# The six-expert part in three groups of 1024 tokens, with 512-column matmuls and results by channel

## The chip, the cores and the metric

The kernel runs on one core of a Trainium2 chip. The metric is the device time of one execution in microseconds, start to end; three executions of the kernel before are given. Besides them there is one execution recorded by the hardware profiler, whose span runs from the first to the last instruction.

## The reference

A decaying linear attention (4 batches, 8 heads, 768 steps, head size 48) produces 3072 tokens of 384 channels. They go into a layer of 8 experts:

```python
logits = x @ w_gate                       # 3072 x 384 by 384 x 8
P = np.exp(logits - logits.max())
for _ in range(8):                        # rows and columns scaled in turn
    P /= P.sum(1, keepdims=True) + 1e-09
    P /= P.sum(0, keepdims=True) + 1e-09
    P *= N / E
out = np.zeros((N, D))
for e in range(E):
    h = np.maximum(x @ w1[e], 0.0)        # 384 -> 1024
    out += P[:, e:e + 1] * (h @ w2[e])    # 1024 -> 384
```

All experts see all tokens; P weighs their results. P is known only when the last token is, since its columns run over all tokens.

## The kernel before

**Precision.** A float32 operand of a matmul is held as two halves of a shorter format, a high one and a low one (`hh` and `hl`, `xh` and `xl`, index 0 and 1 of X and of the weight tiles). Each matrix product is three matmuls: high by high, high by low, low by high.

**Two parts.** In the first part (up to 593 us) the attention runs in chunks of 256 tokens, and the matmuls of experts 0 and 1 (L263 to L293) fill TensorE in between, weights resident, moving operand of 256 columns in the first layer and 384 in the second. A planner (class `Plan`) puts all its operations in an order, by costs and ranks; a job's cost in microseconds is the second argument of `job`. The order is then written out as it stands. Results of experts 0 and 1 go to DRAM without P (`ye_d`).

**Six experts.** The second part does experts 2 to 7 in groups of `UN` = 768 tokens, four groups (`u`), each in 16 steps (`t`, `NT`); a step is three blocks of 128 hidden channels. Tokens of a group are split in two halves of 384 (`TH`, index `j`). The first layer of a step, a 3x3 by 3x2 block product, is done with 15 products of 128x128 by 128x384 instead of 18, by sums of weight blocks and of X blocks formed beforehand; `PRODS` is their order, each adds to one of two PSUM banks A and B in turn, and after each product ScalarE copies the bank or VectorE adds it to or subtracts it from one of six running sums `s11` to `s32`. When a sum is complete, ScalarE writes relu's high half, and VectorE the low half (L1376, L1383). So a bank's content has to be read before the product after next, which goes to the same bank.

**Order in a step.** `step` writes the order out by hand: at position m from 1 to 15 there is the product, then its read, then the list `slots[m]` of other work, then one or two pieces (two at 5, 10 and 15) of the second layer of the step before. A piece is one block of hidden channels for 128 tokens: hidden values are the stationary operand, weights of 384 columns the moving one, three matmuls (L1277 to L1279) into one of six PSUM accumulators. When an expert's eight blocks are done, the accumulator is evicted: in group 0, when P isn't known yet, ScalarE copies it and it goes to DRAM; in the others it is multiplied by P per token and added up in SBUF (L1250, L1252).

**What lies in the slots.** In group 0 the weight sums of the next step (`prep_w`), written to DRAM too (`w_d`) and read back by the later groups (`fetch_w`); the eight scalings of P (`gating`, one round per step), which take a PSUM bank at a step's end for a small matmul; forming X of the next group in the last steps (`load_x`), into tiles that come free by and by; and in the later groups the joining of group 0's stored results (`late`, `join`) and of experts 0 and 1 (`fetch`, `mixin`). Weight tiles hold four to a step: a and b and a part of c the 15 sums, the rest of c and all of d the second layer. There are 10 (`WIDE`) for this part.

**The opening.** X of group 0, the weights of the first two steps and the first 15 products are planned into the first part's end (`opening`), between the last matmuls of experts 0 and 1.

All DMAs are issued from SyncE's queue, in program order. TensorE, VectorE and ScalarE each run their own instructions in program order.

Of the kernel before, what the change touches and what calls it, by code (L numbers as in the profile page):

```python
# [18 lines left out]
CH = 128  # L19
# [6 lines left out]
WIDE = 10  # L26
# [3 lines left out]
UN = 768  # L30
# [96 lines left out]
class Net:  # L127
# [9 lines left out]
    def build(self):  # L137
# [3 lines left out]
        with ExitStack() as ctx:  # L141
            dram = ctx.enter_context(tc.tile_pool(name="dram", bufs=1, space=DR))
            cst = ctx.enter_context(tc.tile_pool(name="cst", bufs=1))
            self.wp = ctx.enter_context(tc.tile_pool(name="wp", bufs=WIDE))
            self.psA = ctx.enter_context(tc.tile_pool(name="psA", bufs=2, space=PS))
# [22 lines left out]
            self.ye_d = [[dram.tile([128, C], F32, name=f"ye_d{u}_{i}") for i in range(self.ntt) if u < 2 or i < NS * NCH] for u in range(E)]  # L168
# [88 lines left out]
    def experts(self, i):  # L257
# [37 lines left out]
        for e in range(2):  # L295
            for f in range(NF):
# [4 lines left out]
                job("PE", 1.07, lambda e=e, f=f, p=p: first(e, f, p), xr + w1, [b], 10 * n)  # L301
# [14 lines left out]
    def phase1(self, c1, ca):  # L316
# [4 lines left out]
        self.wy = c1.enter_context(tc.tile_pool(name="wy", bufs=RING - WIDE))  # L321
# [44 lines left out]
        self.xs, self.plan, self.expert, self.seconds = {}, Plan(), set(), {}  # L366
# [360 lines left out]
    def opening(self, K):  # L727
# [9 lines left out]
        self.X, self.W, self.raw, self.home, self.H = {0: {}}, {}, {}, {}, {}  # L737
        self.nraw, self.nprep, self.want = [0, 0], 0, None
        X, t, L = self.X[0], {}, {}

        def tile(tag, name, wr=False):
            return (self.wr if wr else self.xa).tile([128, TH], F32, tag=tag, name=name)

        ring = ["y0", "y1", "xs", "mo0", "my0", "mo1", "my1"]
# [6 lines left out]
        def whole(k, c, j):  # L751
            tag = turn()

            def load():
                t[c, j], L[c, j] = tile(f"oa{k}", f"xt0{c}{j}_0"), tile(tag, f"xt1{c}{j}_0", tag == "xs")
# [3 lines left out]
            job("SP", 0.9, load, (), [("oa", k), ("low", tag)], land=6.0, kb=384)  # L759
            job("DVE", 0.475, lambda: V.tensor_tensor(t[c, j], t[c, j], L.pop((c, j)), ADD), [("low", tag)], [("oa", k), ("x", c, j)])  # L760

        def new(n):
            tag = spot[n]
            X[n] = self.xa.tile([128, 2, TH], F32R, tag=tag, name=f"X{n}_0")
            self.home[0, n] = (self.xa, tag)
            return X[n]

# [858 lines left out]
```

## Time and profile before

| | |
|---|---|
| median of three runs | 1706.25 us (1702.0 to 1706.36) |
| profiled execution, span | 1699.2 us; the page gives no other time of it, and the runs lie 2.8 to 7.2 us above its span |
| TensorE busy | 1672.3 us, 98%, 13776 matmuls |
| VectorE busy | 1281.3 us, 75% |
| ScalarE busy | 803.1 us, 47% |
| GpSimd busy | 8.9 us |
| DMA, mean share of the 16 engines | 59% |
| part with six experts | 593.5 to 1693.6 us |

Matmuls overlap in their records (one of 384 columns is shown with 334 ns and the next starts 173 ns after it), so their rate is read from starts, not from durations. The same holds for VectorE: its recorded durations are longer than the distance of two starts.

### The profile page before, as it was taken

The page shows a single profiled execution, that of the slowest core. Times are in us where ns is not written, and L with a number is a line of the kernel's source. Part 1 is how long each engine was busy: PE and PEld are TensorE (multiplying, and loading weights), DVE is VectorE, ACT ScalarE, POOL GpSimd, SP SyncE. Part 2 cuts the span into 40 slices and gives each one's busy share as a digit, 9 for nine tenths or more (in the row PEclk, how much of TensorE's full clock was granted, in tenths as well). Part 3 has the DMA queues.
Part 4 walks back from the last instruction along what each step waited for, and adds up shares of the span by engine and source line. Part 5 has one row for each costly group of instructions (what it writes and reads, how often), then busy time and mean ns, then how long its engine had stood idle before and what let it go on. Part 6 is the DMA issues. An engine that isn't in the chain of part 4 may idle for free.

```text
span 1699.2 us, 35042 instructions
## 1 busy us (share of the span) xinstructions
PE 1672.3 (98%) x13776; PEld 1631.4 (96%) x13776; DVE 1281.3 (75%) x2942; ACT 803.1 (47%) x1866; POOL 8.9 (1%) x20
## 2 busy tenths in 40 slices
PE   6999999999999999999999999999999999999998
PEld 3899999999999999999999999999999999999998
DVE  8899989999994989999854767665566766465665
ACT  7766656656553655555543333333333333333332
POOL 1000000000000000000000000000000000000000
PEclk9999999999999999999999999999999999999999
DMA  7445555445545888788875565666465566555460
GB/s 228 124 116 136 125 131 130 118 118 131 130 105 151 261 320 299 272 277 293 305 263 215 198 229 193 257 239 240 178 224 204 214 250 222 211 193 211 183 245 35
DMA packets 163469, 338.79 MB, mean 199 GB/s; under 512 B 14880, under 2 KB 122848, under 8 KB 163296
## 3 DMA queue, kind: packets, MB, share of 16 engines
q1 hardware_dynamic: 162496, 336.08, 59.0%
q8 instruction: 110, 1.80, 0.4%
q14 instruction: 63, 0.52, 0.1%
q10 hardware_dynamic: 800, 0.39, 0.1%
HBM read 236.27 MB, written 81.20 MB: 187 GB/s over the span
## 4 chain that ended last, share of the span: by engine, by line


## 5 line engine op out<-in xcount | busy, mean ns | idle before, releaser
L1376 ACT ACTIVATE hh<-s 128x384 fp32r<-128x384 f32 x378 | 198.9, 526 | 413.7 <-DVE s L1372 373.2
L1372 DVE TENSOR_TENSOR s<-s,A 128x384 f32<-128x384 f32 x315 | 174.0, 552 | 139.5 <-PE A L1358 137.0
L1279 PE MATMUL po<-w_d,hl 128*128 128x384 f32 x768 | 256.6, 334 | 0.0
L1278 PE MATMUL po<-w_d,hh 128*128 128x384 f32 x768 | 256.6, 334 | 0.0
L1277 PE MATMUL po<-w_d,hh 128*128 128x384 f32 x768 | 256.6, 334 | 0.0
L1383 DVE SCALAR_TENSOR_TENSOR hl<-s,hh 128x384 fp32r<-128x384 f32 x378 | 208.7, 552 | 6.1
L267 PE MATMUL ph<-xh,w 128*128 128x256 f32 x576 | 165.7, 288 | 1.2 <-ACT hl L273 0.8
L269 PE MATMUL ph<-xh,w 128*128 128x256 f32 x576 | 162.3, 282 | 0.0
L268 PE MATMUL ph<-xl,w 128*128 128x256 f32 x576 | 162.2, 282 | 0.0
L1369 ACT ACTIVATE s<-B 128x384 f32<-128x384 f32 x189 | 92.9, 491 | 117.7 <-PE B L1358 114.4
L1372 DVE TENSOR_TENSOR s<-s,B 128x384 f32<-128x384 f32 x189 | 104.1, 551 | 53.9 <-PE B L1358 51.6
L1277 PEld LDWEIGHTS po<-w_d,hh 128*128 128x128 f32 x768 | 144.2, 188 | 0.0
L1278 PEld LDWEIGHTS po<-w_d,hh 128*128 128x128 f32 x768 | 144.2, 188 | 0.0
L1279 PEld LDWEIGHTS po<-w_d,hl 128*128 128x128 f32 x768 | 144.2, 188 | 0.0
L273 ACT ACTIVATE hh<-ph 128x256 fp32r<-128x256 f32 x192 | 73.5, 383 | 131.2 <-PE ph L269 130.7
L285 PE MATMUL po<-w,hh 128*128 128x384 f32 x384 | 131.6, 343 | 0.0
L286 PE MATMUL po<-w,hh 128*128 128x384 f32 x384 | 128.9, 336 | 0.0
L287 PE MATMUL po<-w,hl 128*128 128x384 f32 x384 | 128.8, 336 | 0.0
L1279 PE MATMUL po<-w_c,hl 128*128 128x384 f32 x384 | 128.3, 334 | 0.0
L1278 PE MATMUL po<-w_c,hh 128*128 128x384 f32 x384 | 128.3, 334 | 0.0
L1277 PE MATMUL po<-w_c,hh 128*128 128x384 f32 x384 | 128.3, 334 | 0.0
L1391 DVE TENSOR_TENSOR s<-s,B 128x384 f32<-128x384 f32 x63 | 34.9, 554 | 115.7 <-PE B L1358 115.7
(258 smaller groups left out, 4075.7 us busy)
## 6 DMA issues: line engine op xcount, KB each, us to landing
w_d<-w_d SPq DMA_DIRECT2D x64, 768.0 KB, 7.2
w_a<-w_d SPq DMA_DIRECT2D x48, 768.0 KB, 4.3
w_b<-w_d SPq DMA_DIRECT2D x48, 768.0 KB, 5.7
w_c<-w_d SPq DMA_DIRECT2D x48, 768.0 KB, 6.3
raw<-in_w_dram SPq DMA_DIRECT2D x32, 576.0 KB, 5.8
w_d<-w_a SPq DMA_DIRECT2D x16, 768.0 KB, 3.2
w_d<-w_b SPq DMA_DIRECT2D x16, 768.0 KB, 5.0
w_d<-w_c SPq DMA_DIRECT2D x16, 768.0 KB, 6.3
```

What stands on the lines that cost most here:

```text
L267: nc.tensor.matmul(p, w[:, 0, cs], xh[:, ct, :], start=(ct == 0), stop=False)
L268: nc.tensor.matmul(p, w[:, 0, cs], xl[:, ct, :], start=False, stop=False)
L269: nc.tensor.matmul(p, w[:, 1, cs], xh[:, ct, :], start=False, stop=(ct == NCT - 1))
L285: nc.tensor.matmul(o, hh[:, s], w2h, start=f == 0, stop=False)
L286: nc.tensor.matmul(o, hh[:, s], w2l, start=False, stop=False)
L287: nc.tensor.matmul(o, hl[:, s], w2h, start=False, stop=f == NF - 1)
L1277: nc.tensor.matmul(po[k], hh[:, s], w2[:, 0], start=c == 0, stop=False)
L1278: nc.tensor.matmul(po[k], hh[:, s], w2[:, 1], start=False, stop=False)
L1279: nc.tensor.matmul(po[k], hl[:, s], w2[:, 0], start=False, stop=c == NF - 1)
L1372: V.tensor_tensor(S[nm], S[nm], ps, op)
L1376: A.activation(hh, S[nm], AF.Relu)
L1383: V.scalar_tensor_tensor(hl, S[nm], 0.0, hh.bitcast(F32), ALU.max, ALU.subtract)
```

## The change

Groups of the six-expert part get 1024 tokens (`UN`), so there are three, and halves 512. All products and second-layer matmuls have a moving operand of 512 columns.

The second layer turns its operands round: a block of 128x128 weights is stationary, the hidden values of 512 tokens move, and the result stands by channel. A piece is now one block of hidden channels, one half of tokens and one third of the channels; `TURNS` is the order of (block, half) in a step. The factors of P can't be applied per partition at the eviction any more. They are written to DRAM by token (`g_d`) and loaded, the same in every partition, as a tile per expert and half; in groups 1 and 2 VectorE multiplies them in right after a sum is complete (maximum with 0, then the factor), and ScalarE copies the high half from that. With that, an accumulator can run over all six experts in PSUM and is evicted once per group. In group 0 it is evicted per expert as before, and joined later with factor tiles (`pull`, `join`).

Results of experts 0 and 1 still stand by token; they are mixed by token, transposed in blocks of 32 on VectorE and stored so that DRAM holds them by channel (`mix`, `b_d`), and are the base to which groups add. The output leaves by channel, and the host's rearrangement at the end restores its order.

X of a group exists once. The sums of the next group are formed from step 3 on and stored to DRAM (`forms`, `xf_d`); in the last step of a group each X tile is rewritten right after the product that used it last. Weight tiles become 8; the four others of the ring of the first part hold four X tiles of three planes, whose third planes are low halves of the hidden values. The second half of d is therefore made at the beginning of the next step.

```diff
-WIDE = 10
+WIDE = 8
 LAG = 3
 TR = 4
 TB = 32
-UN = 768
+UN = 1024
 TH = UN // 2
 NS = UN // SUB
 NT = 6 * NF // 3
-NX = 15
+NX = 11
 WOPS = [2, 8, 6, 1, 12, 14, 3, 4, 7, 13, 10, 11, 0, 9, 5]
+ROWS = (1, 2, 0)
+TURNS = [(2, 1), (2, 0), (0, 0), (0, 1), (1, 1), (1, 0)]
...
+            self.u_d = {(e, k): dram.tile([128, TH], F32, name=f"u_d{e}_{k}") for e in range(2, E) for k in range(2 * NCT)}
+            self.b_d = [[dram.tile([C, TH], F32, name=f"b_d{u}_{j}") for j in range(2)] for u in range(self.N // UN)]
+            self.g_d = dram.tile([self.ntt, E, CH], F32, name="g_d")
...
+        ring = ["y0", "y1", "mo0", "xh", "xl", "my0"]
+        held = [self.firsts[self.N // (NCH * CH) - 2]]
...
+            if spot[n] < NX:
+                X[n] = self.xa.tile([128, 2, TH], F32R, tag=f"x{spot[n]}", name=f"X{n}_0")
+            else:
+                o = self.wy.tile([128, 3, TH], F32R, tag="w", name=f"X{n}_0")
+                X[n] = o[:, :2]
+                self.tail.append(o[:, 2])
             return X[n]
+
+        def lot(n):
+            k = spot[n] = len(spot)
+            return [self.seconds[1, k - NX]] if k >= NX else []
...
+        g = yield from bank([half, 2, CH])
+        for q in range(2):
+            nc.tensor.transpose(g[:, q], flat[:, half * q:half * q + half], self.ident)
+        V.tensor_copy(pt, g)
+        nc.sync.dma_start(self.g_d.rearrange("(q t) e c -> (t e) q c", q=2), pt)
+        yield
...
+        def factor(o, u, j, e):
+            g = self.g_d[NS * u * NCH + j, e]
+            nc.sync.dma_start(wide(o), bass.AP(g.tensor, g.offset, [[0, 128], [NCH * E * CH, NS], [1, CH]]))
...
+        def mix(tt, part):
+            y0, y1 = Y[tt]
+            if part == 0:
+                A.activation(y0, y0, AF.Copy, scale=self.P[:, tt, 0:1])
+            elif part == 1:
+                V.scalar_tensor_tensor(y0, y1, self.P[:, tt, 1:2], y0, ALU.mult, ALU.add)
+            else:
+                m = late("m", f"m{tt}", None, C)
+                V.transpose(m, y0)
+                u, r = divmod(tt, NS * NCH)
+                s, j = divmod(r, NCH)
+                for b in range(4):
+                    nc.sync.dma_start(self.b_d[u][j][:, s * CH + 32 * b:s * CH + 32 * b + 32].rearrange("(q a) b -> a q b", a=32), m[32 * b:32 * b + 32].rearrange("a (q b) -> a q b", b=32))
...
+        def join(q):
+            if q >= len(pairs):
+                return
+            k, e = pairs[q]
+            (y, g), o = J.pop((k, e)), J["o", k]
+            V.tensor_tensor(y, y, g, ALU.mult)
+            V.tensor_tensor(o, o, y, ALU.add)
+            if e == E - 1:
+                nc.sync.dma_start(result(0, k), wide(o))
...
-            if e == 2:
-                oa[tt] = self.xa.tile([128, C], F32, tag=f"oa{k}", name=f"oa{tt}")
-                A.activation(oa[tt], po[k], AF.Copy, scale=self.P[:, tt, 2:3])
-            else:
-                V.scalar_tensor_tensor(oa[tt], po[k], self.P[:, tt, e:e + 1], oa[tt], ALU.mult, ALU.add)
-            if e == E - 1:
-                nc.sync.dma_start(self.out[tt * CH:tt * CH + CH, :], oa[tt])
+            o = oa[u, k]
+            V.tensor_tensor(o, o, po[k], ALU.add)
+            nc.sync.dma_start(result(u, k), wide(o))
...
+            for i, j in TURNS:
+                for c in range(NCT):
+                    yield u, 2 + (3 * t + (i + 1) % 3) // NF, u * NT + t, i, j, NCT * j + c
...
-            nc.tensor.matmul(po[k], hh[:, s], w2[:, 0], start=c == 0, stop=False)
-            nc.tensor.matmul(po[k], hh[:, s], w2[:, 1], start=False, stop=False)
-            nc.tensor.matmul(po[k], hl[:, s], w2[:, 0], start=False, stop=c == NF - 1)
-            if c == NF - 1:
+            c = k % NCT
+            nc.tensor.matmul(po[k], w2[:, 0, c], hh, start=f == 1, stop=False)
+            nc.tensor.matmul(po[k], w2[:, 0, c], hl, start=False, stop=False)
+            nc.tensor.matmul(po[k], w2[:, 1, c], hh, start=False, stop=f == last)
...
+            if 1 < n < NT:
+                _, hi, lo, _ = prep[n]
+                slots[1] += [hi(5)]
+                slots[4] += [lo(5)]
+            elif n >= NT:
+                slots[1].append(lambda: self.fetch_w(n, [3]))
+            if n + 1 < NT:
+                def begin():
+                    prep[n + 1] = self.prep_w()
+
+                slots[1].append(begin)
+
+                def do(q, *a):
+                    return lambda: prep[n + 1][q](*a)()
+
+                slots[1] += [do(0, 0, 3)]
+                slots[2] += [do(0, 3, 8)]
+                slots[3] += [do(0, 8, 13), do(1, 0)]
+                slots[4] += [do(1, 1)]
+                slots[5] += [do(2, 0)]
+                slots[6] += [do(1, 2), do(1, 3), do(2, 1)]
+                slots[7] += [do(2, 2), do(2, 3)]
+                slots[9] += [do(1, 4)]
+                slots[13] += [do(2, 4)]
+            elif n + 1 < len(steps):
+                slots[1].append(lambda: self.fetch_w(n + 1, [0, 1]))
+                slots[6].append(lambda: self.fetch_w(n + 1, [2]))
...
+            if u + 1 < NU and t == NT - 2:
+                for q in range(3):
+                    slots[13 + q].append(lambda: (deal(len(jobs)), [ahead(u + 1) for _ in range(3 if jobs else 2)]))
+            if u + 1 < NU and t == NT - 1:
+                for m, (c, k) in enumerate(PRODS, 1):
+                    if k in self.plains:
+                        slots[m].append(lambda k=k: self.fetch_x(u + 1, k))
+                    else:
+                        slots[m].append(lambda k=k: A.activation(X[k][:, 0], queue[k], AF.Copy))
+                        (slots[m + 1] if m < 8 else carry).append(lambda k=k: (V.tensor_tensor(X[k][:, 1], queue[k], X[k][:, 0].bitcast(F32), ALU.subtract), ahead(u + 1)))
...
+                if t == 0 and u > 1:
+                    for k in range(2 * NCT):
+                        slots[1 + k].append(lambda k=k: ground(u - 1, k))
+                a, b = divmod(n - 1, NT)
+                if a and (3 * b + 3) // NF > 3 * b // NF:
+                    a, b = divmod((E - 2) * a + 3 * b // NF + 2, E - 2)
+                    if a < NU:
+                        slots[3].append(lambda: factors(a, 2 + b))
+                for m, q in zip((3, 6), joins(n)):
+                    slots[m].append(lambda q=q: join(q))
+                for m, q in zip((11, 13), joins(n + 1)):
+                    slots[m].append(lambda q=q: pull(q))
...
+                h[i, j] = halves(i, j, n)
+                if u:
+                    V.scalar_tensor_tensor(S[nm], S[nm], 0.0, G[u, 2 + (3 * t + (i + 1) % 3) // NF, j], ALU.max, ALU.mult)
+                A.activation(h[i, j][0], S[nm], AF.Copy if u else AF.Relu)
...
+                    if u:
+                        V.tensor_tensor(hl, S[nm], hh.bitcast(F32), ALU.subtract)
...
-                4: lambda ps: (add("s22", ps), high(1, 1, "s22")),
+                4: lambda ps: add("s22", ps),
                 0: lambda ps: (add("s12", ps, SUB), high(0, 1, "s12")),
-                6: lambda ps: (s21(ps), high(1, 0, "s21")),
+                6: s21,
             }
-            lowers.append(low(1, 0, "s21"))
+            lowers.append(lambda: (high(1, 0, "s21"), low(1, 0, "s21")()))
             slots[9].insert(0, low(2, 1, "s32"))
             slots[10].insert(0, low(0, 0, "s11"))
             slots[11].insert(0, low(2, 0, "s31"))
-            slots[14].insert(0, low(1, 1, "s22"))
-            slots[15].insert(0, low(0, 1, "s12"))
+            slots[14].insert(0, lambda: high(1, 1, "s22"))
+            slots[15][:0] = [low(1, 1, "s22"), low(0, 1, "s12")]
...
+            for k in range(2 * NCT):
+                ground(NU - 1, k)
...
-    out = nc.dram_tensor("out_0_dram", (N, C), F32, kind="ExternalOutput").ap()
+    out = nc.dram_tensor("out_0_dram", (N // CH, 128, NCT, CH), F32, kind="ExternalOutput").ap()
```

## Rows read from the trace of the kernel before

**Rows 1.** The page, section 1: busy us, share of the span, instructions.
```profile
PE 1672.3 (98%) x13776; PEld 1631.4 (96%) x13776; DVE 1281.3 (75%) x2942; ACT 803.1 (47%) x1866; POOL 8.9 (1%) x20
```

**Rows 2.** Table by stretches: us, busy us of each engine (started), PEclk, DMA share, GB/s.
```profile
600.00:700.00 100.00, 99.71 (x572) 98.27 (x572) 90.90 (x237) 55.31 (x112) 0.00 (x0) 1.00 0.85 305
...
1400.00:1500.00 100.00, 100.00 (x579) 100.00 (x578) 55.66 (x106) 36.90 (x72) 0.00 (x0) 1.00 0.58 219
```

**Rows 3.** Waits of TensorE, 590 to 1699 us: total, times, longest.
```profile
PE B L1356 <- DVE s L1372: 0.3, 1, 0.3
```

**Rows 4.** Timeline of TensorE: start us, us, operation; both ends of an undisturbed stretch.
```profile
1111.82 0.34 PE L1357 MATMUL B<-X,w_b 128*128 128x384 f32 x1
...
1248.75 0.34 PE L1279 MATMUL po<-w_d,hl 128*128 128x384 f32 x1
```

**Rows 5.** Timeline of TensorE in the two-expert part, seven periods apart.
```profile
514.80 0.28 PE L267 MATMUL ph<-xh,w 128*128 128x256 f32 x1
...
529.59 0.28 PE L267 MATMUL ph<-xh,w 128*128 128x256 f32 x1
```

**Rows 6.** Timeline of TensorE: first and last matmul of the six-expert part's steps.
```profile
593.50 0.33 PE L1356 MATMUL B<-X,w_b 128*128 128x384 f32 x1
...
1693.27 0.34 PE L1279 MATMUL po<-w_c,hl 128*128 128x384 f32 x1
```

**Rows 7.** Timeline of TensorE around one pair of the gating's matmuls.
```profile
699.31 0.34 PE L1279 MATMUL po<-w_d,hl 128*128 128x384 f32 x1
699.48 0.28 PE L1157 MATMUL g<-cs,ones 128*128 128x8 f32 x2
...
700.03 0.34 PE L1357 MATMUL B<-X,w_b 128*128 128x384 f32 x1
```

**Rows 8.** DMA issues: queue, count, KB each, median us to landing.
```profile
X<-x_d SPq DMA_DIRECT2D x32, 192.0 KB, 5.3
```

**Rows 9.** Timeline of VectorE, operations back to back.
```profile
557.48 0.55 DVE L777 TENSOR_TENSOR xs<-xt,xs 128x384 f32<-128x384 f32 x1
557.95 0.55 DVE L784 TENSOR_TENSOR X<-xs,X 128x384 fp32r<-128x384 f32 x1
...
565.98 0.95 DVE L1086 TENSOR_TENSOR w_a<-sum,w_a 128x768 fp32r<-128x768 f32 x1
566.85 0.42 DVE L277 TENSOR_TENSOR hl<-hf,hh 128x256 fp32r<-128x256 f32 x1
```

**Rows 10.** Groups of instructions by line and form: busy us, mean ns; idle before.
```profile
L1252 DVE SCALAR_TENSOR_TENSOR oa<-po,P,oa 128x384 f32<-128x384 f32 x90 | 53.7, 613 | 25.0 <-PE po L1279 25.0
```

**Rows 11.** Table by stretches: within group 0, and across groups 1 and 2.
```profile
700.00:820.00 120.00, 120.00 (x693) 119.71 (x693) 110.88 (x303) 66.15 (x133) 0.00 (x0) 1.00 0.78 274
...
1111.00:1249.00 138.00, 138.00 (x796) 137.53 (x794) 82.22 (x160) 50.51 (x99) 0.00 (x0) 1.00 0.61 224
```

**Rows 12.** Timelines of TensorE and VectorE: from product to read, and back.
```profile
618.33 0.33 PE L1358 MATMUL B<-X,w_a 128*128 128x384 f32 x1
618.70 0.56 DVE L1391 TENSOR_TENSOR s<-s,B 128x384 f32<-128x384 f32 x1 [1.28 <-PE B L1358]
...
622.48 0.55 DVE L1372 TENSOR_TENSOR s<-s,B 128x384 f32<-128x384 f32 x1
623.09 0.44 PE L1356 MATMUL B<-X,w_b 128*128 128x384 f32 x1 [0.25 <-DVE s L1372]
```

**Rows 13.** Table by stretches, the opening: first stretch and sum.
```profile
545.00:555.00 10.00, 10.00 (x76) 9.91 (x74) 3.02 (x8) 3.89 (x11) 0.00 (x0) 1.00 0.98 290
...
sum 48.00, PE 48.00 PEld 47.91 DVE 39.36 ACT 27.77 POOL 0.00; mean PE 9.60 PEld 9.58 DVE 7.87 ACT 5.55 POOL 0.00
```

**Rows 14.** DMA issues: the last stores.
```profile
out_dram<-oa SPq DMA_DIRECT2D x18, 192.0 KB, 1.9
```

**Rows 15.** Line of the raw weights' loads: durations, and time to landing.
```profile
L1035 SPq DMA_DIRECT2D raw<-in_w_dram x32: 383/406/1728, 527.7 to 820.5; - x32
...
DMA to landing us min/median/max: 4.3/5.8/7.9
```

More of the change, by code (lines that the diff above doesn't have):

```diff
@@ L875, in opening @@
         plain(11, *x31)
-        plain(0, *x22)
         raw(1)
@@ L879, in opening @@
         gates(1)
+        plain(0, *x22)
         lower(2)
@@ new lines, in run @@
+                o = self.xf_d[u, n] = self.dram.tile([128, TH], F32, name=f"xf_d{u}_{n}")
+                nc.sync.dma_start(o, low[f])
+            out.append(run)
+        ADD, SUB = ALU.add, ALU.subtract
+        r, l = regs, low
+        load(0, 0, 0, 0)
+        load(1, 0, 1, 1)
+        whole(0, 0)
+        whole(1, 1)
+        load(0, 1, 2, 1)
+        form(3, 0, r[0], r[1], SUB)
+        whole(2, 1)
+        form(8, 0, r[0], r[2], ADD)
+        form(12, 1, r[1], l[0], SUB)
+        load(1, 1, 3, 0)
@@ L1047, in prep_w @@
         self.nprep += 1
-        ts = self.slots(n)
+        ts = self.slots(n, range(2) if inline else range(4))
         raw = self.raw.pop((0, n))
@@ L1134, in gating @@
         cs = sp.tile([128, E], F32, name="cs")
+        half = self.ntt * E // 2
+        pt = sp.tile([half, 2, CH], F32, name="pt")
         V.tensor_reduce(mx, flat, AX.X, ALU.max)
@@ new lines, in base, with late, factors, fetch @@
+        def base(u, k):
+            j, c = divmod(k, NCT)
+            return self.b_d[u][j][c * 128:c * 128 + 128, :]
+        def late(tag, name, bufs=None, n=TH):
+            return more["pool"].tile([128, n], F32, tag=tag, name=name, bufs=bufs)
+        G = {}
+        def factors(u, e):
+            for j in range(2):
+                G[u, e, j] = late(f"g{j}", f"g{u}_{e}_{j}", 2)
+                factor(G[u, e, j], u, j, e)
+        Y = {}
+        def fetch(tt):
+            Y[tt] = [late(f"y{q}", f"y{q}_{tt}", 2, C) for q in range(2)]
@@ new lines, in phase2b, with pull @@
+        pairs = [(k, e) for k in range(2 * NCT) for e in range(2, E)]
+        J = {}
+        def pull(q):
+            if q >= len(pairs):
+                return
+            k, e = pairs[q]
+            if e == 2:
+                J["o", k] = late("jo", f"jo{k}")
+                nc.sync.dma_start(J["o", k], base(0, k))
+            J[k, e] = late("jy", f"jy{k}_{e}", 2), late("jg", f"jg{k}_{e}", 2)
+            nc.sync.dma_start(J[k, e][0], self.u_d[e, k])
+            factor(J[k, e][1], 0, k // NCT, e)
@@ L1287, in step @@
                 for i, j, nm in ((2, 1, "s32"), (1, 1, "s22"), (0, 1, "s12")):
-                    hh, hl = (hp.tile([128, TH], F32R, tag=f"{q}{i}{j}", name=f"{q}{i}{j}_0", bufs=2) for q in ("hh", "hl"))
+                    hh, hl = halves(i, j, 0)
                     A.activation(hh, self.sums[nm], AF.Relu)
@@ L1331, in deal @@
+            for m in (2, 4, 7, 8, 10, 12):
+                slots[m].append(lambda: next(gate, None))
             def deal(k):
```

414 lines of the change are left out of this document (190 added, 224 removed).

## The prediction

> **What bounds the kernel now.** I read the busy shares first, then the table by stretches, then TensorE's waits, and only then the order of single instructions. TensorE is busy for 1672.3 of 1699.2 us, VectorE for 1281.3 [rows 1]. A busy share alone proves little, because matmuls overlap; the table shows more: from 600 to 1600 us, 572 to 579 matmuls start in each 100 us, whatever the other engines do, and the granted clock is 1.00, that is 2.4 GHz [rows 2]. TensorE's waits between 590 and 1699 us that the profile can name sum to 0.3 us [rows 3]. So the six-expert part is bound by how fast matmuls follow one another. That rate has its own rows: between two undisturbed points 790 matmuls of 384 columns take 136.93 us, 173.33 ns each [rows 4]. 384 columns at 2.4 GHz are 160.0 ns; 13.3 ns per matmul are not columns.
>
> **The change part by part.**
>
> *Fewer, wider matmuls.* One step before issues 15 products and 18 second-layer pieces of three matmuls each, 99 matmuls of 384 columns, over 4 x 16 steps: 6336. After it is the same 99 per step, of 512 columns, over 3 x 16 steps: 4752. The columns are equal (2,433,024 both times), so what goes is the part of a matmul that isn't columns, 1584 times. No row has a 512-column matmul of this kind. The two nearest sizes are 384 and, in the two-expert part, 256: seven periods of nine 256-column and six 384-column matmuls last 529.59 - 514.80 = 14.79 us [rows 5], 2.113 a period; less 6 x 0.1733 there remain 1.073 for nine, 119.2 ns each, 12.5 over its 106.7 of columns. The excess hardly grows: 12.5 at 256, 13.3 at 384. Continued on that line it is 14.1 at 512 (pitch 227.4); held at 13.3 the pitch is 226.7. I take 227.0 between them. Before: 6336 x 0.17333 = 1098.2 us. After: 4752 x 0.2270 = 1078.7. **-19.5 us**; -17.5 and -21.1 at the two pitches. The far bound is an excess that grows with the columns: 173.33 x 512/384 = 231.1 ns and no gain at all.
>
> The Trainium skill (TensorE: Matmul & The Clock Gate, Back-to-back issue gap) says that warm matmuls follow one another after their columns at 2.4 GHz plus a fixed 2.5 ns or so. By that, an estimate from the page, the change would save only 1584 x 2.5 ns = 4.0 us. This trace has 13.3 ns where the page has 2.5 [rows 4], in a stream in which each matmul loads weights of its own, and the measurement decides.
>
> *What else TensorE loses.* From 593.50 to the end of the last matmul's turn (1693.27 + 0.17) are 1099.9 us [rows 6]; the 6336 - 45 matmuls issued there take 1090.4 of them, the other 45 being issued before, in the opening. Of the 9.5 left, the gating's own small matmuls take about 4: one such place goes from 699.31 to 700.03, 0.72 us where two plain turns are 0.35, so 0.37 [rows 7], and there are 11. The new transposes make it 12. The other 5 or so lie where groups change: three changes become two, about -1. New there: X is now one set, rebuilt in the last step of a group, ScalarE's copy directly after the product that used the tile, from a prefetch issued three products earlier, behind the last sums. A load of X took 5.3 us in the middle [rows 8]; from slot 13 of one step to slot 1 of the next are about 5.4, so the first copy may hold ScalarE by a microsecond, twice: +1 to +2. Sum **+1**, bounds -3 (all of the rest gone) and +4.
>
> *VectorE's load.* It is paid only if it makes TensorE wait. VectorE's turn is shorter than its recorded duration: 128x384 operations start 0.47 us apart, a 128x768 one 0.87 after which the next starts [rows 9], so 512 columns take 0.47 + 128 x 0.40/384 = 0.60. A step of groups 1 and 2 has 10 sums from PSUM, 6 low halves and, new, 6 gating products: 22 x 0.60 = 13.2 us. VectorE's evictions with the factor go (30 per group, 613 ns each [rows 10]; 6 more are ScalarE's); in their place there are 6 per group, 0.2 us a step. Joins of group 0 cost 72 operations over 21 steps, 3.4 x 0.60 = 2.1; mixing two of 0.47; forming X about 1.1. Sum 17.6 us in a step of 99 x 0.227 = 22.5: 78%. Group 0 before is busy for 110.88 of 120 us [rows 11], 16.0 of a 17.3 us step, and TensorE loses nothing but the gating's turns; its 16 operations of 384 columns grow by 0.13 each (2.1) and X takes about 1 more: 19.1 in 22.5, 85% where it was 92%. So the cover holds on average.
>
> What counts is each single read of PSUM. A product's bank is needed again ten matmuls after the start of its last one. Before that is 1.73 us; VectorE starts to read 0.37 us after that matmul starts, takes 0.55, and TensorE follows 0.06 after [rows 12], so a read may be 0.75 us late. After: 2.27 - (0.37 + 0.05 + 0.67 + 0.06) = 1.1 us. The new gating product stands directly behind the sum on VectorE, and the next read behind both. At positions 8 and 9 this makes 1.2 + 1.8 us of work in 2.7 of TensorE's, at 14 and 15 1.8 + 1.8 in 3.4: lag up to 0.4, less than 1.1. One step is worse, the first of group 2, where six evictions (3.6 us) and six late halves of X (3.6) fall in: 13.2 + 3.6 + 3.6 + 0.9 = 21.3 of 22.5, with a lag of about 1.2 at the last read. I put **+0.5** on it (0 to 3). The copies of relu's result on ScalarE now wait for VectorE's gating product; their readers stand a slot or more behind, and ScalarE is busy for only 50.51 of 138 us there [rows 11]. I cost it at nothing.
>
> *Opening.* After the last logits TensorE has 48 us of two-expert work and products, without a gap, while VectorE is 39.4 of 48 us busy [rows 13]. 33 operations become 0.13 us longer: 4.4 us. VectorE's idle time lies mostly ahead of 555 (3.0 of 10 us busy), where it waits for loads, and two of the temporaries now wait for the last-but-one chunk. Four of the X tiles wait for second-layer weights of the second expert; behind the fourth there are still four rounds of 2.1 us each. Cover is there, not much: **+1** (0 to +6).
>
> *Tail.* Last sum 0.1 us longer, and a store of 256 KB in 512-byte pieces where one of 192 KB in 1536-byte pieces took 1.9 us [rows 14]: **+0.6** (0 to +2).
>
> *At nothing:* weight traffic (3 MB a step, for 22.5 us instead of 17.3, so the DMA share of 0.61 [rows 11] falls), the order of weight rows, the extra output transposition, the two-expert part.
>
> Sum: -19.5 + 1 + 0.5 + 1 + 0.6 = -16.4. The profiled execution's span is 1699.2, and by this 1682.8 after; the runs shown lie 2.8 to 7.2 above that span, the median 7.05, so I take it from the median: 1706.25 - 16.4 = 1690.
>
> **Rivals.**
> *A, wider matmuls save nothing.* The excess grows with columns (231.1 ns). For it: no 512-column row. Against: 256 columns would then have 8.9 ns of excess and have 12.5. Time: 1706.25 + 3.1 = 1709. Chance 0.08. The Trainium skill's constant of 2.5 ns (the section named above) would give nearly the same, 1706.25 - 4.0 + 3.1 = 1705, an estimate from that page.
> *B, slower: VectorE's reads come late in groups 1 and 2.* It decides once a read lags more than 1.1 us. If at three places of each of the 32 steps (9, 10, 15) the product behind comes 0.4 us late, that is 38 us: 1728; from 0.22 us at each the gain is gone and the kernel is over the 0.3% bound. For it: two thirds of the steps get six more operations on VectorE in the very chain. Against: 78% load and a longer grace than before. Chance 0.07.
> *C, weights just in time.* With 8 weight tiles instead of 10, the second half of a step's second-layer weights is made at the start of the next step, and the raw load behind it has from slot 4 to slot 9. It starts about 1.8 us into slot 4 and is wanted 9.6 us after that slot's start: 7.8. Loads took 4.3, 5.8 in the middle, 7.9 at most [rows 15]. If it misses by 0.5 to 1 us in all 14 steps, +7 to +14: 1697 to 1704. Chance 0.08.
>
> **How the numbers follow.** Forecast 0.77, A 0.08, B 0.07, C 0.08. The forecast's own range is 1684 (-21.1, -1) to 1698 (-17.5, with the upper bounds of two of the other terms). The 8-in-10 range reaches over most of C: 1682 to 1703. About 0.3% (5 us) is what a measurement can tell from none; faster by more, that is under 1701: 0.77 + 0.06 of C = 0.83. Within: A and the end of C, 0.10. Slower: B, 0.07.
>
> **What would show it.** Right: the 512-column matmuls start 0.227 us apart, about 440 in 100 us; no wait of TensorE on VectorE over 1 us outside the first step of group 2 and the group changes; the last logits stay at about 545. Wrong: 0.231 apart (A); repeated waits of TensorE on sums at positions 9, 10 and 15 from about 950 us on (B); ScalarE waiting for raw weights in group 0 (C); a gap of TensorE at 590 to 600 (the opening).

## The result, and the profile after

After: 1728.0 us, the median of 4 runs (1722.49 to 1729.72), beside 1704.13 for the kernel before (1702.0 to 1706.36, 4 runs). The ratio is 1.0139, with an interval of 1.0117 to 1.0162: slower by about 24 us where 16 less were forecast. The span of the profiled execution is 1728.0 us, against 1699.2 before. One execution of a kernel further down, no_gate, took 5828 us for a reason that no run shows, and stands in no figure here.

The page of the changed kernel, busy time and DMA packets, to be read beside [rows 1]:

```profile
PE 1661.1 (96%) x12194; PEld 1431.1 (83%) x12194; DVE 1361.7 (79%) x2815; ACT 763.8 (44%) x1679; POOL 9.0 (1%) x20
...
DMA packets 239183, 329.77 MB, mean 191 GB/s; under 512 B 53808, under 2 KB 189616, under 8 KB 239024
```

No other engine has become the bound: VectorE went from 75% to 79%, and TensorE from 98% down to 96%. TensorE now waits. The wanted saving is there all the same. An undisturbed stretch of TensorE's timeline, as [rows 4]:

```profile
1004.17 0.39 PE L1343 MATMUL po<-X,w_c 128*128 128x512 f32 x1
...
1179.84 0.39 PE L1344 MATMUL po<-hh,w_c 128*128 128x512 f32 x1
```

775 turns lie between these two: 175.67 us, 226.67 ns each. At 2.4 GHz that is 213.33 of columns and again 13.3 of something else.

TensorE's waits in the six-expert part, where [rows 3] had one line of 0.3 us (us in total, times, longest):

```profile
PE B L1449 <- ACT s L1460: 9.5, 2, 5.0
PE A L1449 <- DMA w_c<-w_d: 7.6, 3, 4.3
PE A L1449 <- DMA oa<-b_d: 7.2, 1, 7.2
PE A L1449 <- DVE s L1463: 2.9, 2, 2.5
PE B L1449 <- DMA w_b<-w_d: 2.3, 1, 2.3
PE A L1449 <- DMA X<-x_d: 2.2, 1, 2.2
PE B L1449 <- DVE s L1484: 1.7, 1, 1.7
PE A L1449 <- ACT s L1460: 1.1, 1, 1.1
```

Four of them name a DMA outright; what the others hide has to be followed. Take the first: it ends at 950.21 on ScalarE's copy L1460. ScalarE's own timeline shows what held that copy:

```profile
941.01 1.15 ACT L1469 ACTIVATE hh<-s 128x512 fp32r<-128x512 f32 x2 [1.45 <-DVE s L1463]
949.04 0.63 ACT L1414 ACTIVATE X<-rmy 128x512 fp32r<-128x512 f32 x1 [6.88 <-DMA rmy<-xf_d]
949.58 0.58 ACT L1460 ACTIVATE s<-B 128x512 f32<-128x512 f32 x1
```

It stood behind the rewriting of X, which waited 6.88 us for a load. And why was that late? SyncE's timeline around it (start, duration of the issuing instruction; x4 sums four):

```profile
929.00 0.38 SPq L1128 DMA_DIRECT2D w_c<-w_d  x1
929.48 1.05 SPq L1550 DMA_DIRECT2D rmo<-xf_d  x1
930.57 5.43 SPq L1245 DMA_DIRECT2D g<-g_d  x4
936.05 2.97 SPq L1266 DMA_DIRECT2D y<-ye_d  x1
939.12 2.23 SPq L1550 DMA_DIRECT2D rmy<-xf_d  x1
...
953.12 9.22 SPq L985 DMA_DIRECT2D X<-x_d  x2
```

The load of `rmy` is issued 3.1 us after the last of four factor loads (L1245) and a 2.97-us issue of `y`, takes 2.23 us to issue itself and lands some 8 us later. An issue takes 0.3 to 0.6 us when nothing is in its way; here the instructions stand still in the act of issuing, up to 9.22 us for a pair. Taken over the whole part the queue is slow. Page section 6 and the view of DMA issues (queue, count, KB each, median us to landing):

```profile
w_a<-w_d SPq DMA_DIRECT2D x32, 768.0 KB, 7.1
w_b<-w_d SPq DMA_DIRECT2D x32, 768.0 KB, 8.7
w_c<-w_d SPq DMA_DIRECT2D x32, 768.0 KB, 11.3
...
jg<-g_d SPq DMA_DIRECT2D x36, 256.0 KB, 12.9
...
g<-g_d SPq DMA_DIRECT2D x24, 256.0 KB, 11.6
```

Before, the three weight loads took 4.3, 5.7 and 6.3. The 60 factor loads (`g`, `jg`) are new and the slowest of these, though they are a third of a weight load in size. As late as they are only the loads of `jy`, which are issued in between them (12.2), and the stores of `jo` (12.8). The table by stretches, 950 to 1650 us (columns as [rows 2]):

```profile
950.00:1650.00 700.00, 670.11 (x2900) 550.18 (x2901) 504.80 (x796) 216.84 (x366) 0.00 (x0) 0.98 0.72 217
```

The DMA share is 0.72, where the kernel before has 0.58 in the same stretch. The bytes are the same (217 and 216 GB/s).

The longest wait, 7.2 us, bears the name of `oa<-b_d`, but a product doesn't read `oa`. VectorE's timeline shows whom it waits for, and SyncE's shows why:

```profile
1531.87 0.69 DVE L1302 TENSOR_TENSOR jo<-jo,jy 128x512 f32<-128x512 f32 x1 [9.41 <-DMA jo<-b_d]
1532.48 0.68 DVE L1463 TENSOR_TENSOR s<-s,A 128x512 f32<-128x512 f32 x1
...
1509.88 2.69 SPq L1304 DMA_DIRECT2D out_dram<-jo  x1
...
1529.29 0.34 SPq L1291 DMA_DIRECT2D jo<-b_d  x1
```

The read of bank A (L1463), for which the product waits, stands on VectorE behind a join (L1302) that waits for a new `jo`. This load is issued only when the store of the old `jo` has landed, at 1529.23, 19.4 us after its issue. The wait of 2.5 us that bears VectorE's name (at 1234.50) has the same path, and that of 1.7 us stands behind VectorE's L1005, which waits 3.54 us for a store of `rf`. The last line, 1.1 us, hides no DMA; the part on the prediction comes back to it.

A wait of several us costs more than itself. TensorE's timeline after the longest one:

```profile
1525.58 0.39 PE L1344 MATMUL po<-hh,w_c 128*128 128x512 f32 x1
1533.21 0.80 PE L1449 MATMUL A<-X,w_c 128*128 128x512 f32 x1 [7.25 <-DMA oa<-b_d]
1533.81 0.63 PE L1450 MATMUL A<-X,w_c 128*128 128x512 f32 x1
1534.23 0.63 PE L1451 MATMUL A<-X,w_c 128*128 128x512 f32 x1
```

The matmuls behind the gap start 0.43 us apart in place of 0.227, which is the 1.2 GHz level (the granted clock of 1525 to 1535 us is 0.75); seven turns later they are back. Some forty such turns in the part cost about 8 us.

**The ledger.** From the first matmul of the part's steps to its last: before, 593.50 to 1693.27 with 6291 matmuls at 173.33 ns, after, 601.41 to 1720.15 with 4707 at 226.67 ns (the 45 first products of each lie in the opening). What the count times the pitch doesn't explain is "lost".

| us | before | after | difference |
|---|---|---|---|
| the part's steps begin | 593.5 | 601.4 | +7.9 |
| matmuls at their pitch | 1090.4 | 1066.9 | -23.5 |
| lost between them | 9.5 | 52.0 | +42.5 |
| behind the last matmul | 5.8 | 7.6 | +1.9 |
| span | 1699.2 | 1728.0 | +28.8 |

### The profile page after: what moved, and what is told of

Same layout as the page of the kernel before. It is cut to its first block, busy times and chain, and to the rows that moved or that the text cites. A ratio compares the mean times of both kernels' runs of the same rounds, so it can differ in the third digit from the quotient of the medians.

```text
span 1728.0 us, 31712 instructions
## 1 busy us (share of the span) xinstructions
PE 1661.1 (96%) x12194; PEld 1431.1 (83%) x12194; DVE 1361.7 (79%) x2815; ACT 763.8 (44%) x1679; POOL 9.0 (1%) x20
## 2 busy tenths in 40 slices
DMA packets 239183, 329.77 MB, mean 191 GB/s; under 512 B 53808, under 2 KB 189616, under 8 KB 239024
## 5 line engine op out<-in xcount | busy, mean ns | idle before, releaser
L1469 ACT ACTIVATE hh<-s 128x512 fp32r<-128x512 f32 x282 | 175.3, 631 | 467.5 <-DVE s L1468 352.2
L1342 PE MATMUL po<-hh,w_d 128*128 128x512 f32 x576 | 225.0, 391 | 0.3 <-ACT st L1309 0.3
L1344 PE MATMUL po<-hh,w_d 128*128 128x512 f32 x576 | 225.1, 391 | 0.0
L1463 DVE TENSOR_TENSOR s<-s,A 128x512 f32<-128x512 f32 x235 | 160.6, 684 | 54.8 <-PE A L1451 51.1
L1343 PE MATMUL po<-X,w_d 128*128 128x512 f32 x432 | 169.0, 391 | 0.0
L1460 ACT ACTIVATE s<-B 128x512 f32<-128x512 f32 x141 | 84.5, 599 | 120.2 <-PE B L1451 115.3
L1468 DVE SCALAR_TENSOR_TENSOR s<-s,g 128x512 f32<-128x512 f32 x192 | 129.7, 689 | 4.4
L1342 PEld LDWEIGHTS po<-hh,w_d 128*128 128x128 f32 x576 | 108.6, 188 | 23.5 <-ACT st L1309 0.8
L1344 PEld LDWEIGHTS po<-hh,w_d 128*128 128x128 f32 x576 | 108.6, 189 | 22.7
L1463 DVE TENSOR_TENSOR s<-s,B 128x512 f32<-128x512 f32 x141 | 96.3, 683 | 27.7 <-PE B L1451 27.3
L1344 PE MATMUL po<-hh,w_c 128*128 128x512 f32 x288 | 112.9, 392 | 0.0
L1342 PE MATMUL po<-hh,w_c 128*128 128x512 f32 x288 | 112.9, 392 | 0.0
L273 PEld LDWEIGHTS ph<-xh,w 128*128 128x128 f32 x576 | 108.6, 189 | 3.6 <-ACT hl L279 1.1
L275 PEld LDWEIGHTS ph<-xh,w 128*128 128x128 f32 x576 | 109.1, 189 | 0.0
L274 PEld LDWEIGHTS ph<-xl,w 128*128 128x128 f32 x576 | 108.9, 189 | 0.1
## 6 DMA issues: line engine op xcount, KB each, us to landing
w_c<-w_d SPq DMA_DIRECT2D x32, 768.0 KB, 11.3
```

The source lines that it names most:

```text
L273: nc.tensor.matmul(p, w[:, 0, cs], xh[:, ct, :], start=(ct == 0), stop=False)
L274: nc.tensor.matmul(p, w[:, 0, cs], xl[:, ct, :], start=False, stop=False)
L275: nc.tensor.matmul(p, w[:, 1, cs], xh[:, ct, :], start=False, stop=(ct == NCT - 1))
L1342: nc.tensor.matmul(po[k], w2[:, 0, c], hh, start=f == 1, stop=False)
L1343: nc.tensor.matmul(po[k], w2[:, 0, c], hl, start=False, stop=False)
L1344: nc.tensor.matmul(po[k], w2[:, 1, c], hh, start=False, stop=f == last)
```

## The experiments

In all twelve, "lost" is the third line of this ledger. By the order of instructions, SyncE issues the same DMAs in the same order as in the changed kernel in all that touch only the factors' loads (f_pool apart, and the store of the factors where it is split), so that order is no cause here.

| kernel | factor loads | us, median | ratio to before (interval) | lost |
|---|---|---|---|---|
| changed | 512 x 512 B, 8192 B apart | 1728.0 | 1.0139 (1.0117 to 1.0162) | 52.0 |
| wide_mix | as changed | 1708.25 | 1.0034 (1.0017 to 1.0051) | 32.8 |
| wide_factors | 128 x 2 KB | 1686.19 | 0.9909 (0.9888 to 0.9929) | 8.6 |
| wide_both | 128 x 2 KB | 1693.18 | 0.9941 (0.9918 to 0.9963) | 11.8 |
| no_gate | as changed | 1742.11 | 1.0208 (1.0170 to 1.0246) | 62.3 |
| pad | 512 x 512 B, 576 B apart | 1688.73 | 0.9934 (0.9908 to 0.9960) | 9.0 |
| gate_wide | g 2 KB, jg as changed | 1706.55 | 1.0025 (1.0008 to 1.0042) | 22.1 |
| join_wide | jg 2 KB, g as changed | 1696.40 | 0.9966 (0.9952 to 0.9980) | 17.6 |
| f_pool | as changed, POOL's queue | 1734.14 | 1.0182 (1.0160 to 1.0203) | 59.5 |
| stores24 | as changed | 1734.97 | 1.0184 (1.0158 to 1.0210) | 59.5 |
| stride9k | 512 x 512 B, 9216 B apart | 1684.09 | 0.9899 (0.9882 to 0.9916) | 6.3 |
| stride16k | 512 x 512 B, 16384 B apart | 1747.70 | 1.0280 (1.0243 to 1.0317) | 69.9 |
| spread | 512 x 512 B, 8192 B apart, not the same for all | 1684.82 | 0.9892 (0.9875 to 0.9908) | 6.6 |

### First round: which of the additions

The theory after reading the traces was that small pieces stop up the queue (S); its rivals were loads that come just in time (J) and VectorE's gating products (V, the prediction's rival B, whose 1728 us the result happens to equal).

wide_mix: the mixed results of experts 0 and 1 are stored in one DMA with pieces of 512 bytes (in an order that permutes them).

```diff
-                for b in range(4):
-                    nc.sync.dma_start(self.b_d[u][j][:, s * CH + 32 * b:s * CH + 32 * b + 32]..., m[32 * b:32 * b + 32]...)
+                nc.sync.dma_start(self.b_d[u][j][:, s * CH:s * CH + CH].rearrange("(q p) c -> p q c", p=128), m.rearrange("p (q c) -> p q c", c=CH))
```

> Edit: the transposed results of experts 0 and 1 are stored with one DMA per 128 tokens in pieces of 512 bytes, where the changed kernel uses four DMAs in pieces of 128 bytes; the blocks land at other places, so the part of experts 0 and 1 in the result is permuted. Same bytes, same instructions on the compute engines. Theory S (small pieces: the DMA queue is filled by many short pieces, loads behind them land late, and TensorE waits): TensorE's lost time after the opening, 52 us in the changed kernel, falls by 15 to 30, total 1698 to 1713. Theory J (just in time: one set of X, 8 weight tiles and loads asked for a few positions ahead make the waits, whatever the pieces): at most 5 us less, 1723 or more. Theory V (VectorE's gating products are late): no change, 1725 to 1730.

wide_factors: the factors lie so that the four runs of a load are one row of 2 KB; wide_both has both edits.

```diff
-            self.g_d = dram.tile([self.ntt, E, CH], F32, name="g_d")
+            self.g_d = dram.tile([self.N // UN, NCH, E, NS, CH], F32, name="g_d")
...
-            nc.sync.dma_start(wide(o), bass.AP(g.tensor, g.offset, [[0, 128], [NCH * E * CH, NS], [1, CH]]))
+            nc.sync.dma_start(o, bass.AP(g.tensor, g.offset, [[0, 128], [1, TH]]))
```

(The factors are also stored by 24 DMAs in place of one; stores24 below tests this by itself.)

> Edit: the factors of P lie in DRAM so that the 512 of an expert and a half are contiguous; each of the 60 factor loads is then 128 pieces of 2 KB where it was 512 pieces of 512 bytes (they landed after 12 us in the middle). Everything else as in the changed kernel. Theory S: the factor loads land in under 8 us, and 10 to 20 us of the 52 go, total 1708 to 1718. Theory J: at most 5 us less. Theory V: no change.

> Edit: both of the edits before (experts 0 and 1 permuted again). Theory S: nearly all waits on DMAs in groups 1 and 2 go, lost time 10 to 20 us where it was 52, total 1685 to 1697. Theory J: the waits at the group changes (X prefetched three positions ahead, about 20 us with the slow clock behind them) and for weights stay, total 1715 or more. Theory V: 1725 to 1730.

no_gate: the six gating products of a step in groups 1 and 2 are left out (their results aren't scaled).

```diff
-                if u:
-                    V.scalar_tensor_tensor(S[nm], S[nm], 0.0, G[u, 2 + (3 * t + (i + 1) % 3) // NF, j], ALU.max, ALU.mult)
-                A.activation(h[i, j][0], S[nm], AF.Copy if u else AF.Relu)
+                A.activation(h[i, j][0], S[nm], AF.Relu)
...
```

> Edit: VectorE's gating product behind each complete sum is left out in groups 1 and 2 (P is not applied there); ScalarE takes relu's high half from the sum and VectorE the low half, as in group 0. The factor loads stay. 192 VectorE operations of 0.6 us less. Theory V: the 44 us that the changed kernel loses beyond the one before go, total about 1685 to 1692. Theories S and J: VectorE was waiting itself, the waits stay where they are, 1718 to 1728.

V finds no support: without the products VectorE has 192 operations less and the kernel is slower still (1742, above both of the ranges that the theories gave). This run alone doesn't settle it, because in no_gate SyncE issues some loads and stores in another order, at about a dozen places. What settles it is that wide_factors has all the products and not the loss. The factors' layout alone takes 42 us away, all of the loss and the predicted time besides, far more than the 10 to 20 that theory S gave it. The store of the mix takes 20 away while the factor loads stay as they are (12.6 us to landing), and nothing once they are mended: wide_both is 7 us slower than wide_factors alone. This fits a store that relieves a queue which something else has stopped up.

Was it the pieces? wide_factors changed two things at once: the size of a piece, and where the runs lie.

### Second round: pieces, place, or queue

pad keeps the pieces of 512 bytes and puts the four runs 576 bytes apart.

```diff
-            self.g_d = dram.tile([self.ntt, E, CH], F32, name="g_d")
+            self.g_d = dram.tile([self.N // UN, NCH, E, NS, CH + 16], F32, name="g_d")
...
+            nc.sync.dma_start(wide(o), bass.AP(g.tensor, g.offset, [[0, 128], [CH + 16, NS], [1, CH]]))
```

> The factors lie as in wide_factors (a row of four runs for each chunk and expert), but with 64 spare bytes behind each run of 128 tokens, so a load takes 4 pieces of 512 bytes for each partition again (512 pieces a load). SP issues everything in the same order as in the changed kernel and in wide_factors. Theory S (the pieces of 512 bytes are what holds up SP's queue): the waits come back, 1720 to 1735 us, 40 to 55 us lost in the expert part beyond the pitch. Theory L (not the pieces but where the runs lie: in the changed kernel the four runs of a load are 8 KB and more apart): 1683 to 1692 us as wide_factors, about 9 us lost.

1688.73 us: theory S falls. There are as many packets as in the changed kernel, and 176 more, and the loss is gone:

```profile
DMA packets 239359, 329.77 MB, mean 196 GB/s; under 512 B 53984, under 2 KB 189792, under 8 KB 239200
```

gate_wide and join_wide store the factors in both layouts; the one loads `g`, the other `jg` as rows of 2 KB (`if n == "g"`, or `"j"`, ahead of the old load).

> Two copies of the factors are stored; the 24 loads for the gating products (line 1245, tile g) take 128 pieces of 2 KB, the 36 loads for the joins (tile jg) stay at 512 pieces of 512 bytes. Order on SP unchanged. Theory S by the count of small pieces: 24 of 60 loads, so 40% of the 42 us between the changed kernel (1728) and wide_factors (1686) come back: about 1711 us. Theory X (only the loads that stand close before X's reload matter, and these are the g loads at 929 to 955 us): 1690 to 1698 us.

> The other half: the 36 loads for the joins (tile jg) take 128 pieces of 2 KB, the 24 for the gating products stay at 512 pieces of 512 bytes. Theory S by the count: 60% of the 42 us come back, about 1703 us. Theory X (only the g loads ahead of X's reload matter): 1716 to 1724 us, little gained.

Each half brings a good part of the gain (21 and 32 us of 42), with more for the larger number of loads. Neither theory's number is met: by its count of pieces S gave 1711 and 1703, and X gave 1690 to 1698 and 1716 to 1724. The two gains add up to more than the 42 of both together. So both kinds of load cost time, not those beside X's rewriting alone; how much a single load costs isn't shown.

f_pool issues the factor loads, unchanged, from POOL.

```diff
-            nc.sync.dma_start(wide(o), bass.AP(g.tensor, g.offset, [[0, 128], [NCH * E * CH, NS], [1, CH]]))
+            nc.gpsimd.dma_start(wide(o), bass.AP(g.tensor, g.offset, [[0, 128], [NCH * E * CH, NS], [1, CH]]))
```

> The changed kernel with its 60 factor loads, still in 512 pieces of 512 bytes, issued by POOL, which is idle in this part, on a queue of its own. Theory Q (SP's one queue: the loads that stand behind a slow factor load wait for it): the weights and X no longer stand behind them, 1685 to 1700 us, 8 to 20 us lost beyond the pitch. Theory E (the small pieces cost time on the 16 shared DMA engines, whichever queue they come from): 1715 to 1735 us, 35 to 55 us lost.

1734.14 us. A queue of their own doesn't help the others: the factor loads land in 11.7 and 11.9 us, and `w_b` and `w_c` in 8.7 and 12.6 without a factor load ahead of them on SyncE's queue. This points to something that both queues share. The run isn't as clean as the others: on POOL's queue the page counts 4800 packets for these loads, where SyncE's has 31,680 fewer than in the changed kernel, and a few of SyncE's own loads stand in another order; what POOL's own issuing costs, no run shows.

### Third round: the place

stores24 stores the factors in the old places with 24 DMAs, as wide_factors and pad do. stride9k and stride16k keep the one store and only put spare bytes behind each run:

```diff
-            self.g_d = dram.tile([self.ntt, E, CH], F32, name="g_d")
+            self.g_d = dram.tile([self.ntt, E, CH + 16], F32, name="g_d")
...
-        nc.sync.dma_start(self.g_d.rearrange("(q t) e c -> (t e) q c", q=2), pt)
+        nc.sync.dma_start(self.g_d[:, :, 0:CH].rearrange("(q t) e c -> (t e) q c", q=2), pt)
...
-            nc.sync.dma_start(wide(o), bass.AP(g.tensor, g.offset, [[0, 128], [NCH * E * CH, NS], [1, CH]]))
+            nc.sync.dma_start(wide(o), bass.AP(g.tensor, g.offset, [[0, 128], [NCH * E * (CH + 16), NS], [1, CH]]))
```

(stride16k has 128 in place of 16.)

> The factors lie as in the changed kernel (the four runs of a load 8,192 bytes apart), but are stored by 24 small DMAs as in wide_factors and pad; the loads are unchanged. Theory L (where the four runs of a load lie decides): 1720 to 1735 us, as the changed kernel. Theory W (what helped wide_factors and pad was the store, or what it moved in the order or the memory): 1683 to 1695 us.

> The store stays one DMA, the loads stay 512 pieces of 512 bytes; only 64 spare bytes behind each run make the distance of a load's four runs 9,216 bytes in place of 8,192. Theory A (the distance of exactly 8,192 bytes puts the four runs, which all 16 engines read 128 times at once, where they get in each other's way): 1683 to 1695 us, about 9 us lost. Theory D (runs some KB apart are slow at any distance, and only runs close together are quick, as the 576 bytes of pad): 1718 to 1735 us, 40 us and more lost.

> As stride9k with 512 spare bytes behind each run: the four runs of a load lie 16,384 bytes apart. Theory A: slow as at 8,192 or slower, 1720 to 1745 us. Theory D: slow too, 1718 to 1735 us. Theory W' (any change of the factor array's size that moves the other arrays in memory helps): 1683 to 1695 us.

Theory A holds, but for a size: 1728 and 1735 at 8192 bytes with either store, 1684 at 9216, and 1748 at 16384, some 3 us above the range that it gave. Theory D falls by stride9k, and that a mere shift of the other arrays in memory helps (W') by stride16k. 64 bytes of padding are worth 44 us. The landing times of the same loads show it (median us to landing). stride16k:

```profile
w_c<-w_d SPq DMA_DIRECT2D x32, 768.0 KB, 11.8
...
jg<-g_d SPq DMA_DIRECT2D x36, 256.0 KB, 12.7
...
g<-g_d SPq DMA_DIRECT2D x24, 256.0 KB, 12.8
```

stride9k:

```profile
w_c<-w_d SPq DMA_DIRECT2D x32, 768.0 KB, 6.1
...
jg<-g_d SPq DMA_DIRECT2D x36, 256.0 KB, 4.5
...
g<-g_d SPq DMA_DIRECT2D x24, 256.0 KB, 5.2
```

The same bytes in the same number of packets (239,183 in both) land in 4.5 us and not in 12.7, and the weights behind them in 6.1 and not in 11.8. What the DMA share shows of it is nothing. stride9k, 950 to 1650 us:

```profile
950.00:1650.00 700.00, 698.79 (x3081) 577.82 (x3080) 530.76 (x836) 227.28 (x382) 0.00 (x0) 1.00 0.72 221
```

It is 0.72 as in the changed kernel, with TensorE busy for 698.79 of 700 us. SyncE's issuing instructions in this stretch, added up over the timeline, take 190 us there and 440 in the changed kernel. TensorE's waits from 590 us on in stride9k are down to three lines:

```profile
PE A L1449 <- ACT s L1460: 1.1, 1, 1.1
PE B L932 <- DVE s L946: 1.1, 1, 1.1
PE A L1449 <- DVE s L1463: 0.4, 1, 0.4
```

### Fourth round: does it take the broadcast?

spread keeps the distance of 8192 bytes, but lets each partition read other rows.

```diff
-            g = self.g_d[NS * u * NCH + j, e]
-            nc.sync.dma_start(wide(o), bass.AP(g.tensor, g.offset, [[0, 128], [NCH * E * CH, NS], [1, CH]]))
+            g = self.g_d[j, 0]
+            nc.sync.dma_start(wide(o), bass.AP(g.tensor, g.offset, [[CH, 128], [NCH * E * CH, NS], [1, CH]]))
```

> The factor loads keep their 512 pieces of 512 bytes, their order and the distance of 8,192 bytes between a partition's four runs, but partition p starts 512 bytes behind partition p-1, so that a load reads 88 different runs in place of the same four 128 times (the partitions get factors of other tokens and experts, so the result of the gating is left out of what is computed). Theory H (it takes both: all partitions after the same four runs, and these 8,192 bytes apart): 1683 to 1695 us, factor loads landing in about 5 us as in stride9k. Theory A' (the distance within a partition's four runs is enough): 1720 to 1735 us, landing in about 12 us.

(The rows are 128 + 3 x 16 = 176 different ones, not 88, and the same for all loads of a half.) 1684.82 us; the loads land quickest of all:

```profile
w_c<-w_d SPq DMA_DIRECT2D x32, 768.0 KB, 5.9
...
jg<-g_d SPq DMA_DIRECT2D x36, 256.0 KB, 3.3
...
g<-g_d SPq DMA_DIRECT2D x24, 256.0 KB, 4.7
```

So it takes both: 128 partitions that read the same four runs, and these runs 8192 or 16384 bytes apart. Same runs 576 or 9216 bytes apart do no harm, nor do different runs 8192 apart.

The Trainium skill (DMA: Bandwidth & Descriptors, Latency and other measured facts) has a row on this in another form: copies with a pitch between partitions of 2 MiB and more lose up to half of their rate, 4 KiB of padding gives it back and 192 B don't; it puts it down, unverified, to streams that meet in the same memory channel. Here the distance was only 8 KB, inside a load that all partitions read alike, and 64 bytes behind each run, 1024 in the distance, were enough. This lies between the two paddings of the page, so it doesn't contradict them; that it is the same mechanism, no run shows.

**Open.** No run shows what in the memory the four runs share; distances other than 512 (one row), 576, 8192, 9216 and 16384 bytes weren't tried, so it is open whether powers of two matter or, say, all multiples of 8192. Why no_gate and stores24 are some us slower than the changed kernel, and wide_both than wide_factors, isn't known either.

## Why the prediction was wrong

The step that failed is the one headed "At nothing: weight traffic", with its grounds that 3 MB now have 22.5 us and the DMA share falls. It priced what was taken from the queue and not what was put on it: 60 factor loads of 512 pieces each are named nowhere in the sum. Landings of weights from 4.3 to 6.3 us became 7.1 to 11.3, and the loss of 42.5 us stands in the ledger's line "lost" alone. That the DMA share didn't fall but rose, from 0.58 to 0.72, refutes the ground that was given, but isn't the cause: stride9k has 0.72 too and no loss. stride9k takes it out and leaves the rest of the change as it was, so it is the test of the other steps. Its own span is 1681.3, 17.9 below before; forecast were 16.4.

| step | forecast | stride9k | changed |
|---|---|---|---|
| 4752 wide for 6336 matmuls | -19.5 (-21.1 to -17.5) | -21.1 | -21.1 |
| what else TensorE loses, with VectorE's load | +1.5 (-3 to +7) | -3.2 | +42.5 |
| opening and what lies ahead of it | +1 (0 to +6) | +4.8 | +5.5 |
| tail | +0.6 (0 to +2) | +1.7 | +1.9 |
| sum | -16.4 | -17.8 | +28.8 |

(The ledger's -23.5 and +7.9 hold the opening's 45 wider matmuls, 2.4 us, which the first line counts here.) That stride9k's sum comes out within 1.5 us of the forecast is in part luck: the second line is 4.7 us better than forecast, just beyond its bound, and the third 3.8 worse.

- *Pitch:* right, at the bound of 226.7 ns. The excess doesn't grow from 384 to 512 columns: 13.3 ns at both. Rival A is out. The Trainium skill's 2.5 ns per matmul (TensorE: Matmul & The Clock Gate, Back-to-back issue gap), by which the pitch would be 215.8, doesn't hold for this stream at 226.67. The prediction left out that the section gives this for an isolated gap, and for a stream of weight loads and matmuls about 131 ns at 512 columns; that isn't what was measured here either.
- *VectorE:* nearly right. Its wide operations start 0.60 us apart, as worked out, for instance from 1136.27 to 1138.68 in stride9k (0.61, 0.60, 0.60, 0.60), and in the steps TensorE waits 0.4 us for it by name there. The 1.1 us that bear ScalarE's name are VectorE's too. Ahead of this wait, in stride9k:

```profile
1325.88 1.28 DVE L1313 TENSOR_TENSOR oa<-oa,po 128x512 f32<-128x512 f32 x2
...
1327.79 0.63 ACT L1469 ACTIVATE hh<-s 128x512 fp32r<-128x512 f32 x1 [2.75 <-DVE s L1468]
...
1328.96 0.50 PE L1449 MATMUL A<-X,w_b 128*128 128x512 f32 x1 [1.15 <-ACT s L1460]
```

  The evictions (L1313) of the first step of group 2 hold up VectorE's gating product, ScalarE's copy L1469 waits for it, and the read of the bank stands behind the copy. The prediction had this step (+0.5, 0 to 3), but put the wait of ScalarE's copies at nothing, and it is by these that it came. The waits of 2.5 and 1.7 us on VectorE in the changed kernel don't come back in stride9k. Rival B isn't what happened: its number was hit by chance, and stride9k has all the gating products and none of its late reads.
- *X's rewriting:* forecast +1 to +2 from a load of 5.3 us. In stride9k TensorE loses nothing there. In the changed kernel the two waits of 9.5 us together are on this very path: the first because the load queued behind the four slow factor loads, the second (1332.05) with loads of X in front whose issue took 4.80 us for three. The mechanism was seen, and only the duration of the load was taken from a queue without its new neighbours.
- *Opening:* +4.8 within its bounds. Not all of it is the change's: the last logits come at 546.2 in stride9k and 548.2 in the changed kernel, where the text expected about 545, though the two don't differ up to there. One wait is plain, 1.1 us of L932 on VectorE.
- *Tail:* the last three stores land in 4.4 to 4.5 us, where 1.9 stood in [rows 14]; the term was too small by a microsecond.
- *Rival C*, late raw weights in group 0, didn't come: no wait on them is among TensorE's lines. ScalarE waited for them from 590 us on for 3.8 us in all in stride9k, where it was 3.3 before.

Where could it have been seen? Not in the sizes: a factor load moves 256 KB, and the trace of before moves a tile of 192 KB in 5.3 us [rows 8]. But no row of before has a load that gives all partitions the same few rows, and the prediction bounded the other thing without a row, the 512-column matmul, from both sides. Had it bounded the 60 loads too, the lateness of X and w_c would have been a rival with a price; that it would have found the 12 us, nothing shows.

## What to carry to other kernels

Count every DMA that a change adds, by pieces and by where the pieces lie, before calling traffic free; a load that broadcasts a few runs to all partitions did well here with its runs in one row or 576 or 9216 bytes apart, and badly with 8192 and 16384. When all loads of a queue land late together and their issuing instructions stretch, look for the one kind whose addresses coincide: the DMA share and the bytes looked the same with and without the trouble. And when an edit mends something, split it before naming the cause: wide_factors seemed to prove that small pieces were at fault, and pad showed that they weren't.

## What the runs showed of the hardware

- The 36 loads of `jg`, the same in bytes, packets and order, landed in a median of 12.7 us with their runs 16,384 bytes apart and in 4.5 at 9,216; the DMA engines' busy share was 0.71 and 0.72.
- SyncE's issue of a DMA, mostly 0.3 to 0.6 us, stretched to 9.22 us for a pair while the queue was stopped up, and with the same loads issued by POOL the others were as late (`w_c` 12.6 us, 11.3 from SyncE).
- A matmul with a weight load of its own cost 13.3 ns beyond its columns at 384 and at 512 columns.
- Behind a gap of 7.25 us TensorE ran at the 1.2 GHz level for seven turns (0.43 us each), behind one of 4.52 us for five, and behind one of 2.53 us, at 1234.50, for none.
